# First-parity keys and queries by seven block products ahead of the FFN, values beside FFN chunks 0 and 1

## The chip, the core and the metric

The kernel runs on one core of a Trainium2 chip. The metric is the device time of one execution in microseconds (us); the median of several runs counts. The engines are PE (TensorE: matrix products), DVE (VectorE), ACT (ScalarE), POOL (GpSimd) and SP (SyncE, which only issues transfers). PE reads its operands from on-chip memory (SBUF) and writes sums into eight banks of PSUM of 128 x 512 numbers each; DVE and ACT read and write both.

## What is computed

For 2048 tokens x of 512 channels the kernel mixes an attention with a feed-forward network (FFN). The gate `g` is one number per token.

```python
g = sigmoid((x * gate_w).sum(-1, keepdims=True))
qkv = x @ wqkv                      # 32 heads of 16 channels
idx = pos[:, None] - 2 * arange(8)  # each token looks at 8 tokens, two apart
logits = einsum("bhsd,bhswd->bhsw", q, k[:, :, idx]) * 16 ** -0.5
a = einsum("bhsw,bhswd->bhsd", softmax(logits), v[:, :, idx]) @ wo
b = (gelu(x @ w_gate) * (x @ w_up)) @ w_down      # inner width 1792
out = g * a + (1 - g) * b
```

## The kernel before, in words

Since a token looks only at tokens of its own parity, the 1024 even tokens (parity 0) and the 1024 odd ones (parity 1) are worked through one after the other. Products are made in a 32-bit format of reduced precision, so each operand is split into a high half (a rounded copy, mostly made by ACT) and a low half (what is left, a subtraction, mostly made by DVE); each product of blocks is three matrix products: high by high, low by high, high by low. `split` (L82) does this. PE walks over tiles of 128 tokens (8 in a parity, two blocks of 4) and over the 512 channels in `KC` = 4 chunks.

Opening of parity 0 (L793 to L836). x and the weights of the keys and queries of the first 16 heads (column block 0, "cb 0") are loaded on the queues of SP and ACT and split. PE makes cb 0 with `qkv_mm` (L185): 8 tiles x 4 chunks x 3 = 96 products of 512 columns into eight banks. `take_first` (L196) copies the results from PSUM, half of the copies on ACT and half on DVE, and stores them to DRAM by SP. Then `project(0, 1)` (L223) makes the values (cb 1) for both halves of the heads: 192 products of 256 or 258 columns; ACT copies them and stores them from its own queue, and after the last one L240 to L243 turn the logits z of the gate into g. Beside it run the sums of x that the FFN needs (`sums_x`, L125) and the weights of FFN chunk 0 (`combine`, L420, and `operands`, L429, whose low half is a negated copy on ACT to which a POOL transfer adds the raw weights).

FFN (`ffn`, L623). The inner width is cut into 14 chunks of 128. Gate and up projection of a chunk are a product of 2 x 2 blocks, made with seven block products instead of eight (`gate_up`, L537): sums s1 to s4 of blocks of x, sums t1 to t4 of blocks of the weights; the fourth product of a chunk runs late, in the next chunk (`late`, `fourth`). GELU runs on ACT, the product with the up half on DVE, and the result is split again (`hidden`, L494). The down projection of two chunks is made two chunks later as "pieces" of a chunk (`down`, L510). In chunks 0 and 1, which have no such pieces yet, the pieces are `project_one` (L245): the keys and queries of the other 16 heads (cb 2), 96 products of 512 columns.

Attention (L258 to L386) runs on DVE, for 8 units (4 of each parity): scores, softmax, mix. It is a generator from which the steps of PE's work `pull` a budget (L391), so the order is written by hand. `paced` (L348) ties an instruction's place in the schedule to the last product issued, and the order on each engine is settled when the program is built, by a scheduler with its own estimate of times. Scores of a unit need its keys and queries, softmax needs g, mix needs the values. Loads and stores go through SP's queue, the accumulating ones through POOL's. Parity 1 follows in the same way, then the output projection.

What the prediction's steps touch: the warm-up products (L71), the opening (L793 to L836), `project` and `project_one` (L223, L245), the gates (L240), `gate_up`'s pieces in chunks 0 and 1 (L636), and ACT's work at the passage from chunk 1 to chunk 2 (L442, L447, L471, L474, L570, L586).

## Time and profile before

| | us |
|---|---|
| median of 3 runs | 613.11 (611.63 to 613.8) |
| profiled execution | 612.18 |
| its span, first to last instruction | 610.4 |
| PE busy in the span | 602.1 |
| DVE busy | 515.0 |
| ACT busy | 380.0 |
| POOL busy | 82.8 |

The profile is of one execution. A row of the order of time gives the start (us from the span's first instruction), the duration, the engine, the line of the kernel, the operation, the tile written and the tiles read, the shapes and the number of instructions merged; what stands in brackets is the idle time before it and what ended it. A row of a group has, behind the first bar, the busy time in us and the mean duration of one in ns, behind the second the idle time of the engine just before them. PEld is PE's loading of the fixed operand, which overlaps its products. A busy PE is not a PE at its peak, because products are pipelined and their ends are modelled.

### The profile page before, as it was taken

The page shows a single profiled execution, that of the slowest core. Times are in us where ns is not written, and L with a number is a line of the kernel's source. Part 1 is how long each engine was busy: PE and PEld are TensorE (multiplying, and loading weights), DVE is VectorE, ACT ScalarE, POOL GpSimd, SP SyncE. Part 2 cuts the span into 40 slices and gives each one's busy share as a digit, 9 for nine tenths or more (in the row PEclk, how much of TensorE's full clock was granted, in tenths as well). Part 3 has the DMA queues.
Part 4 walks back from the last instruction along what each step waited for, and adds up shares of the span by engine and source line. Part 5 has one row for each costly group of instructions (what it writes and reads, how often), then busy time and mean ns, then how long its engine had stood idle before and what let it go on. Part 6 is the DMA issues. An engine that isn't in the chain of part 4 may idle for free.

```text
span 610.4 us, 8251 instructions
## 1 busy us (share of the span) xinstructions
PE 602.1 (99%) x2839; PEld 503.6 (83%) x2839; DVE 515.0 (84%) x598; ACT 380.0 (62%) x635; POOL 82.8 (14%) x110
## 2 busy tenths in 40 slices
PE   9999999999999999999999999999999999999996
PEld 7898887888887888888889887888888888888885
DVE  6949686969989788799898898999798979999882
ACT  6654465687677777785375347556865676684722
POOL 0151021121111111101100001111111111101200
PEclk9999999999999999999999999999999999999999
DMA  8398978899979979885579989686877886938615
GB/s 286 116 269 238 308 195 236 250 231 248 263 189 284 238 212 267 222 238 170 188 227 256 315 264 283 159 242 161 246 179 217 204 266 135 274 110 200 88 35 172
DMA packets 85591, 132.48 MB, mean 217 GB/s; under 512 B 8111, under 2 KB 52271, under 8 KB 85550
## 3 DMA queue, kind: packets, MB, share of 16 engines
q1 hardware_dynamic: 63742, 94.27, 47.6%
q0 software_dynamic: 12672, 32.84, 28.7%
q10 hardware_dynamic: 9136, 4.85, 2.7%
q8 instruction: 22, 0.36, 0.3%
q14 instruction: 19, 0.16, 0.1%
HBM read 67.18 MB, written 36.77 MB: 170 GB/s over the span
## 4 chain that ended last, share of the span: by engine, by line
PE 93%; DMA 3%; issue 1%; DVE 1%; ACT 1%; POOL 0%; SPq 0%; POOLq 0%; ACTq 0%
PE p L481 40%; PE acc L191 18%; PE p L521 12%; PE acc L521 12%; PE p L742 5%; PE p L191 4%; PE acc L742 2%; DMA g<-raw 2%; DMA d<-r 1%; DMA raw<-xt 1%; DVE prod L327 0%; ACT g L442 0%; POOL g L443 0%; ACT s L788 0%; ACT lg L307 0%
## 5 line engine op out<-in xcount | busy, mean ns | idle before, releaser
L481 PE MATMUL p<-S,g 128*128 128x512 f32 x672 | 165.7, 389 | 0.0
L481 PEld LDWEIGHTS p<-S,g 128*128 128x128 f32 x672 | 126.1, 188 | 26.2
L481 PE MATMUL p<-A,g 128*128 128x512 f32 x504 | 127.5, 390 | 0.7 <-DMA g<-raw 0.7
L481 PEld LDWEIGHTS p<-A,g 128*128 128x128 f32 x504 | 94.3, 188 | 21.0 <-DMA g<-raw 1.1
L289 DVE TENSOR_TENSOR prod<-kq 128x2048 f32<-128x2048 f32 x32 | 73.2, 2288 | 14.4 <-DMA kq<-kq 5.0
L443 POOL DMA_DIRECT2D g<-raw x42 | 36.3, 864 | 314.8 <-ACT g L442 232.9
L327 DVE TENSOR_TENSOR prod<-v,lg 128x2048 f32<-128x2048 f32 x32 | 73.0, 2281 | 3.9 <-PE p L521 2.1
L292 DVE TENSOR_REDUCE lg<-prod 128x128 f32<-128x2048 f32 x32 | 73.1, 2283 | 0.4
L521 PE MATMUL p<-d,hh 128*128 128x512 f32 x224 | 68.3, 390 | 0.6 <-ACT p L515 0.6
L521 PE MATMUL acc<-d,hh 128*128 128x512 f32 x224 | 59.9, 391 | 0.3 <-DMA d<-r 0.3
L486 ACT ACTIVATE s<-p 128x512 f32<-128x512 f32 x56 | 33.2, 594 | 28.3 <-PE p L481 28.1
L521 PEld LDWEIGHTS acc<-d,hh 128*128 128x128 f32 x224 | 41.9, 188 | 10.1 <-DMA d<-r 1.4
L521 PEld LDWEIGHTS p<-d,hh 128*128 128x128 f32 x224 | 41.9, 188 | 9.7 <-ACT p L515 1.1
L495 DVE TENSOR_TENSOR c<-c 128x512 f32<-128x512 f32 x56 | 38.3, 684 | 11.8 <-ACT c L586 11.2
L442 ACT ACTIVATE g<-raw 128x1024 fp32r<-128x1024 f32 (+1 forms) x42 | 41.3, 982 | 11.2 <-DVE raw L424 9.3
L498 DVE TENSOR_TENSOR hl<-c,hh 128x512 fp32r<-128x512 f32 x56 | 38.4, 685 | 11.1 <-ACT hh L497 10.5
L447 ACT ACTIVATE g<-raw 128x1024 fp32r<-128x1024 f32 (+1 forms) x42 | 41.1, 987 | 9.6 <-PE p L481 9.4
L491 DVE TENSOR_TENSOR c<-p,s 128x512 f32<-128x512 f32 x56 | 38.1, 686 | 10.0 <-PE p L481 10.0
L497 ACT ACTIVATE hh<-c 128x512 fp32r<-128x512 f32 x56 | 35.1, 626 | 16.1 <-DVE c L495 16.0
L521 PE MATMUL p<-d,hl 128*128 128x512 f32 x112 | 42.6, 389 | 0.0
L534 ACT ACTIVATE rt<-p 128x512 f32<-128x512 f32 x48 | 28.2, 594 | 18.8 <-PE p L521 18.2
L331 DVE TENSOR_TENSOR prod<-prod 128x1024 f32<-128x1024 f32 x32 | 39.0, 1220 | 0.4
(147 smaller groups left out, 909.9 us busy)
## 6 DMA issues: line engine op xcount, KB each, us to landing
g<-raw POOLq DMA_DIRECT2D x28, 512.0 KB, 6.0
raw<-wff SPq DMA_DIRECT2D x42, 256.0 KB, 4.1
ws<-g SPq DMA_DIRECT2D x14, 768.0 KB, 5.4
g<-ws SPq DMA_DIRECT2D x14, 768.0 KB, 6.3
r<-wff SPq DMA_DIRECT2D x28, 256.0 KB, 3.9
d<-r POOLq DMA_DIRECT2D x28, 256.0 KB, 6.3
g<-raw POOLq DMA_DIRECT2D x14, 384.0 KB, 4.9
v<-vs SPq DMA_DIRECT2D x8, 512.0 KB, 7.5
```

The source lines that it names most:

```text
L191: LAST[:] = [nc.tensor.matmul(ps[:, :cn], a[:, t], w[:, c0:c0 + cn], start=(kc == 0 and n == 0), stop=(kc == KC - 1 and n == 2))]
L289: paced(nc.vector.tensor_tensor(prod, spans(k, jj), q[:, jj:jj + 2, None, :].to_broadcast([P, 2, W, UC]), op=OP.mult))
L292: nc.vector.tensor_reduce(two_of(lg, jj), prod.rearrange("p j w (h d) -> p (j w) h d", d=DH), axis=AX.X, op=OP.add)
L327: paced(nc.vector.tensor_tensor(prod.rearrange("p j w (h d) -> p (j w) h d", d=DH), spans(v, jj).rearrange("p j w (h d) -> p j w h d", d=D ...
L331: nc.vector.tensor_tensor(prod[:, :, :4], prod[:, :, :4], prod[:, :, 4:], op=OP.add)
L442: nc.scalar.activation(lo, raw, AF.Copy, scale=-1.0)
L447: ins = nc.scalar.activation(hi, raw, AF.Copy)
L481: LAST[:] = [nc.tensor.matmul(ps, w_, a_, start=(start and kc == 0 and n == 0), stop=(kc == 1 and n == 2), skip_group_check=True)]
L495: nc.vector.tensor_tensor(ge, ge, up, op=OP.mult)
L498: nc.vector.tensor_tensor(hl_, ge, hh_.bitcast(F32), op=OP.subtract)
L521: LAST[:] = [nc.tensor.matmul(pp, a[:, ts], w, start=(i == 0 and n == 0 and gr == 0), stop=(i == 1 and n == 2), skip_group_check=True)]
L742: LAST[:] = [nc.tensor.matmul(pa, a, b, start=(first and n == 0), stop=(last and n == 2), skip_group_check=True)]
```

## The change

In the opening of parity 0, keys and queries of all 32 heads are made at once as a product of 2 x 2 blocks (token blocks by channel halves on the x side; channel halves by halves of the heads on the weight side), with seven block products of 24 matrix products each, as in the FFN. `start` holds all of it. The four quarter blocks of the weights are loaded as b11 (two transfers on ACT's queue), b21, b12 and b22 (one of 512 KB each on SP's queue) into tiles that attention uses later. DVE makes t1 to t4 (four subtractions of 128 x 1024) and s1 to s4 (which the FFN uses afterwards), and all of them are split, with the high half on ACT. The partial result U = a11 x b11 is copied by ACT into a second bank, so that a12 x b21 can be added to the copy; results of two further products are kept in SBUF by ACT copies and added by DVE (`join`). The low half of the operands of FFN chunk 0 is now made by DVE.

The order in `start` is: U (first chunk of channels, seven filler products behind its second product, then the rest), a12 x b21, s1 x t1, s2 x t2, s4 x b22, s3 x t3, a22 x t4. The warm-up becomes 16 products of 256 columns. The values of parity 0 take the place of cb 2 as pieces of FFN chunks 0 and 1 (`values`), with the budget for attention that they had before, and the gates follow the last of them. Parity 1 stays as it was.

```diff
-WARM = 31
+WARM = 16
+FILLERS = 7
...
+    def gates(par):
+        nc.scalar.activation(en, z[:, par], AF.Exp, scale=-1.0)
+        nc.vector.tensor_scalar_add(en, en, 1.0)
+        nc.vector.reciprocal(g[:, par], en)
+        nc.vector.tensor_scalar(gc[:, par], g[:, par], -1.0, 1.0, op0=OP.mult, op1=OP.add)
+
+    def values(jj):
+        for hh in range(2):
+            ps = bank(f"acc{(2 * jj + hh) % BT}")
+            qkv_mm(ps, 0, jj, 1, range(KC), (CU, 0)[hh], (WQ, CU)[hh])
+            take(ps, 0, jj, hh, True, tag=None if jj < 5 else "c")
+        pull(2.7)
+        if jj == NP - 1:
+            done.add((0, 1))
+            gates(0)
...
-                pieces = [[lambda jj=jj: project_one(par, jj) for jj in jjs]
+                tile_ = (lambda jj: project_one(1, jj)) if par else values
+                pieces = [[lambda jj=jj: tile_(jj) for jj in jjs]
                           for jjs in (((0, 1), (2, 3), (4, 5), ()), ((6,), (7,), (), ()))[f]]
...
-    project(0, 1, first())
+    def start():
...
+        (xh, xl), (wh, wl) = X[0, 0, 0], KW["b11"][0]
+        mm(U[0], 0, xh, wh, True)
+        mm(U[0], 0, xl, wh)
+        for _ in range(FILLERS):
+            ins = nc.tensor.matmul(U[-1][:, :P], warm[:, :P], warm[:, :P], start=True, stop=True)
...
+        def seed(t):
+            V_.append(bank("p"))
+            nc.scalar.activation(V_[t], U[t], AF.Copy)
+
+        block(U, "a11", "b11", False, seed, (1,))
+        split_x(0, 0, 2)
+        split_x(0, 0, 3)
+        operand("b21", b21, g1b)
...
+        block(V_, "a12", "b21", False, lambda t: put(t, V_[t]))
...
+        for kc in range(2):
+            nc.vector.tensor_tensor(s12[kc], q[kc][2], q[kc][3], op=OP.add)
+            split(nc.vector, *XOP["s1", kc], s12[kc])
+        d = [r for _ in range(4) for r in rooms_of("d", 2)]
+        sub(b11, b12, b11)
+        operand("t1", b11, d[:4])
...
+        block(Z_, "s1", "t1", True, keep_p5)
+        for kc in range(2):
+            sub(s12[kc], s12[kc], q[kc][0])
+            split(nc.vector, *XOP["s2", kc], s12[kc])
+        sub(b11, b22, b11)
+        operand("t2", b11, d[4:])
+        block(U, "s2", "t2", False, keep_u2)
...
+        operand("b22", b22, rooms_of("g0", 3, WA) + rooms_of("c", 1))
...
+        sub(b12, b22, b12)
+        operand("t3", b12, [r for _ in range(3) for r in rooms_of("s", 1)] + rooms_of("c", 1))
+        block(Z_, "s4", "b22", False, lambda t: join(t, Z_[t], u2[t]))
+        sub(b21, b21, b11)
+        operand("t4", b21, g1b)
+        block(U, "s3", "t3", False, lambda t: join(BT + t, U[t], p5[t]))
...
+        block(U, "a22", "t4", False, lambda t: put(BT + t, U[t]))
+        done.update(((0, 0), (0, 2)))
+
+    start()
```

Here `block` runs the 24 matrix products of one block product, tile by tile; `operand` splits 512 columns at a time; `put` is `take_first`; `join` adds the kept partial result and stores keys and queries.

More of the change, by code (lines that the diff above doesn't have):

```diff
@@ L65, in bank @@
         return psum.tile([P, 512], F32, name=tag, bufs=BUFS.get(tag, 1))
[L68 to L80 removed]
+    zero = pool.tile([P, UC], F32, name="zero")
+    nc.vector.memset(zero, 0.0)
+    warm = zero.bitcast(mybir.dt.bfloat16)
+    LAST = []
+    idle = [bank("p") for _ in range(4)]
+    for i in range(WARM):
+        c = i // 4 % 2 * QW
+        LAST[:] = [nc.tensor.matmul(idle[i % 4][:, c:c + QW], warm[:, :P], warm, start=not c, stop=True,
+                                    skip_group_check=True)]
     def split(eng, hi, lo, raw, copy=None):
@@ L790, in finish @@
                 queue.dma_start(out_v[2 * jj + 1, :, c], r[:, c])
-    room = rooms()
-    room_x(0)
-    for kc in range(KC):
-        first = ((0, P), (P, 512 - P)) if not kc else ((0, 512),)
-        sp = load_cb(0, kc, "c", room)
-        if not kc:
-            XR.update((i, tl("raw")) for i in range(2))
-        for blk in range(2):
-            for a, n in first if not blk else ((0, 512),):
-                o = (2 * blk + kc // 2) * 512 + a
-                nc.sync.dma_start(XR[kc % 2][:, o:o + n], xt[blk, :, kc, a:a + n])
-            split_x(0, blk, kc, first if not blk else ((0, 512),), nc.vector.tensor_copy if not (kc or blk) else None)
-            if not blk:
-                sp()
@@ L807, in tile_gated_mix @@
-    ps = [bank(next(names)) for _ in range(NP)]
-    for kc in range(KC):
-        for jj in range(NP):
-            qkv_mm(ps[jj], 0, jj, 0, (kc,))
-    for t in (*KS.values(), *VS.values()):
-        for c in range(2):
-            paced(nc.gpsimd.dma_start(t[c, :W], zero))
-    for jj in range(NP):
-        take_first(ps[jj], jj, nc.vector.tensor_copy if jj % 2 else lambda o, i: nc.scalar.activation(o, i, AF.Copy))
-    done.add((0, 0))
-    for kc in range(KC):
-        load_cb(1, kc, "c", room)()
@@ L829, in first @@
         combine(0)
         for i in range(2):
-            yield
-            for _ in operands(0, 0, i):
-                yield
-        combine(1)
-    project(0, 1, first())
+            n = len(GROUPS[i]) * QW
+            w = tl(f"g{i}", F32R)
+            hi, lo = w[:, :n], w[:, n:2 * n]
+            for k, op in enumerate(GROUPS[i]):
+                WG[0, op] = hi[:, k * QW:(k + 1) * QW], lo[:, k * QW:(k + 1) * QW]
+            split(nc.vector, hi, lo, RAW[0][:, (0, 4)[i] * QW:][:, :n])
```

165 lines of the change are left out of this document (132 added, 33 removed).

## The prediction

> **What bounds the kernel now.** I read the page first: the busy times, then the chain of waits.
>
> ```profile
> span 610.4 us, 8251 instructions
> PE 602.1 (99%) x2839; PEld 503.6 (83%) x2839; DVE 515.0 (84%) x598; ACT 380.0 (62%) x635; POOL 82.8 (14%) x110
> PE 93%; DMA 3%; issue 1%; DVE 1%; ACT 1%; POOL 0%; SPq 0%; POOLq 0%; ACTq 0%
> ```
>
> PE is the bound over the whole span, and 93% of the chain that ended last is PE. So a product less is a gain, and any wait that PE is given is a loss, because nothing later takes it back. Then I cut the first 96 us into the stages that the change touches. The columns are PE, weight loads, DVE, ACT and POOL busy, then clock, DMA share and GB/s.
>
> ```profile
> 4.40:27.50 23.10, 22.59 (x97) 18.18 (x97) 21.20 (x38) 15.23 (x29) 0.00 (x0) 1.00 0.66 221
> 27.50:52.00 24.50, 24.50 (x200) 24.21 (x198) 16.02 (x20) 13.32 (x36) 10.28 (x19) 1.00 0.84 230
> 52.00:84.00 32.00, 32.00 (x143) 26.50 (x142) 25.53 (x24) 13.74 (x21) 2.47 (x3) 1.00 0.93 288
> 84.00:96.00 12.00, 11.67 (x52) 9.30 (x51) 9.64 (x11) 9.16 (x15) 2.60 (x3) 1.00 0.80 184
> ```
>
> The reader should see the first row: while PE makes 96 key and query products, DVE is busy 21.2 of 23.1 us. DVE is nearly full exactly where the change adds DVE work. In the last row ACT is busy 9.2 of 12 us, where before (third row) it had 18 us free.
>
> **The price of a product.** From PE's order of time:
>
> ```profile
> 4.42 0.99 PE L191 MATMUL p<-g,A 128*128 128x512 f32 x2
> 5.91 0.50 PE L191 MATMUL p<-g,A 128*128 128x512 f32 x1 [0.51 <-DVE A L84]
> 16.65 1.52 PE L191 MATMUL p<-S,A 128*128 128x512 f32 x6
> 18.01 1.52 PE L191 MATMUL acc<-S,A 128*128 128x512 f32 x6
> 27.53 1.24 PE L191 MATMUL acc<-g,A 128*128 128x258 f32 x9
> 28.60 0.52 PE L191 MATMUL acc<-c,A 128*128 128x258 f32 x3
> ```
>
> Six 512-column products take 18.01 - 16.65 = 1.36 us, 0.2267 each; nine value products take 1.07, 0.119 each. Keys and queries of the first parity need 192 products before (two heads' halves, 8 token tiles, 4 chunks of channels, 3 for the high and low halves) and 7 x 4 x 2 x 3 = 168 after. **Removed: 24 x 0.2267 = 5.44 us of PE.** The values' 192 products only move. The warm-up (31 of 128 columns, then 16 of 256) is as many columns, and the seven fillers stand in the gap before the row at 5.91, where PE waits for x anyway; I cost both at nothing, -0.2 to +0.3. Without the gap the fillers would cost their own length, under 0.8 us.
>
> **What the opening adds.** The seven products need sums of x and of the weights, and each sum is split in two halves, the high one on ACT and the low one on DVE. The DVE rows that price them:
>
> ```profile
> 6.84 0.69 DVE L87 TENSOR_TENSOR g<-c,g 128x512 fp32r<-128x512 f32 x1
> 13.37 0.68 DVE L87 TENSOR_TENSOR A<-raw,A 128x512 fp32r<-128x512 f32 x1
> 13.97 0.69 DVE L133 TENSOR_TENSOR raw<-raw 128x512 f32<-128x512 f32 x1
> 23.65 0.42 DVE L202 COPY kq<-p 128x256 f32<-128x256 f32 x1
> 23.99 0.41 DVE L203 COPY hl<-p 128x256 f32<-128x256 f32 x1
> L331 DVE TENSOR_TENSOR prod<-prod 128x1024 f32<-128x1024 f32 x32 | 39.0, 1220 | 0.4
> ```
>
> Back to back a 512-wide operation costs 0.60 (13.37 to 13.97), a PSUM copy 0.34, a 1024-wide subtraction 1.22 - 0.08 = 1.14. In the built order of the changed program PE can run 56 products (a11 x b11, a12 x b21, and eight of s1 x t1). The 57th needs the low half of t1 = b12 - b11. On DVE that half stands behind these, counted from the operation that is at 6.84 in both programs: 18 operations of 512 with itself (10.8), the two 1024-wide subtractions t1 and t3 (2.28), and four copies of finished a12 x b21 tiles (1.36). That is 14.4 us if DVE never waits. It waits once for b21, whose arrival I take from these two rows (the second is GB/s in slices of 1.125 us from 0):
>
> ```profile
> 8.27 0.63 ACT L86 ACTIVATE A<-raw 128x512 fp32r<-128x512 f32 x1 [0.99 <-DMA raw<-xt]
> GB/s 0 17 288 249 389 219 339 406 402 380 357 365 316 298 189 0 0 7 0 0 9 232 343 193 154 118 148 276 192 261 259 364 369 371 241 208 204 220 245 259
> ```
>
> The load that ends at 1,280 KB lands at 8.25, and 256 KB more at 400 GB/s are 0.65 us, so b21 lands about 8.9; its high half follows on ACT at 9.5, where DVE would have come at 8.05: 1.5 us, and I add 0.4 for one later wait on ACT. **The half is ready at 6.84 + 14.4 + 1.9 + 0.1 = 23.3 us** (bounds: 21.4 with no wait, 25.0 if DVE waits about as much again). The remaining 112 products take 25.4. PE stands still on the way again: s4 x b22 writes the banks of s1 x t1, and their copies stand on ACT behind a split that waits for DVE (0.6, then 0.3 twice, since a copy is longer than a product), then the high half of t2 (0.5): 1.7, between 0 and 3. Keys and queries end at 23.3 + 25.4 + 1.7 = 50.4.
>
> Both kernels are then compared at the same work. Before, at 52.0, the first half of keys and queries, all values and 6 FFN products are done, and 96 x 0.2267 = 21.8 remain: 73.8. After: 50.4 + 192 x 0.119 (22.9) + 6 x 0.2267 (1.4) = 74.7. **The opening comes out at +0.9**: the 5.44 are spent on waits for DVE. Between the bounds: -2.7 to +3.9. The eight joins (0.60 each), the values' splits and the operands of chunk 0, which change from a POOL DMA to DVE, come after the handover and beside products; they cost nothing as long as DVE is done by about 50, and its queue after 23.3 (some 43 operations, about 27 us) just is. The 18 stores to DRAM on SP and the values' stores on ACT's queue move with their steps; PE waits for neither.
>
> **What the move of the values adds.** The gates need an Exp after the last value. Before, that Exp stood ahead of the FFN; now it stands in chunk 1 between two GELUs, and the softmax's Exp follows. The built order has 21 table loads on ACT instead of 17, three of them at the passage from chunk 1 to 2, where before there was none:
>
> ```profile
> 66.42 1.28 ACT L570 ACT_TABLE_LOAD   x1
> 67.72 0.60 ACT L570 ACTIVATE c<-p 128x512 f32<-128x512 f32 x1
> 50.67 0.21 ACT L240 ACTIVATE en<-z 128x8 f32<-128x8 f32 x1 [0.38 <-ACT z L221]
> 49.84 0.39 ACT L213 ACTIVATE hh<-acc 128x256 f32<-128x256 f32 x1 [1.07 <-PE acc L191]
> 50.12 0.17 ACT L221 ACTIVATE z<-acc 128x1 f32<-128x1 f32 x1
> 63.58 0.62 ACT L307 ACTIVATE lg<-lg 128x512 f32<-128x512 f32 x1
> 83.71 0.60 ACT L586 ACTIVATE c<-p 128x512 f32<-128x512 f32 x1 [0.76 <-PE p L481]
> 88.27 1.79 ACT L447 ACTIVATE g<-raw 128x768 fp32r<-128x768 f32 x2
> L447 ACT ACTIVATE g<-raw 128x768 fp32r<-128x768 f32 x14 | 11.8, 842 | 0.0
> 90.08 1.52 PE L481 MATMUL p<-A,g 128*128 128x512 f32 x6
> 90.28 1.15 ACT L474 ACTIVATE d<-r 128x512 fp32r<-128x512 f32 x2 [0.22 <-PE p L481]
> 91.44 0.39 PE L521 MATMUL acc<-d,hh 128*128 128x512 f32 x1
> 92.16 0.50 PE L521 MATMUL acc<-d,hh 128*128 128x512 f32 x1 [0.33 <-DMA d<-r]
> ```
>
> Before, ACT goes without a break from the GELU at 83.71 to the high halves of chunk 2's operands: the first is ready at 88.27 + 0.84 = 89.1, and PE takes it at 90.08, 1.0 us of room. After, two loads (2.56), the Exp (0.2), a second value copy and z (0.5) stand in between: 3.3 more. PE has 0.6 more work there (24 value products and 19 of 512, 7.2 us, against 29 of 512, 6.6). So PE waits 3.3 - 1.0 - 0.6 = 1.7. Next, PE needs the high half of the down weights. Behind the operands' first half ACT has the third load (1.28), the softmax's Exp (0.53 back to back), the second operand (0.95) and that copy (0.63): 3.4, and PE has six products (1.4) to run: 2.0 more. Less the 0.33 that PE waits at this place already, **the passage costs +3.4**, between 0 and 4.5.
>
> [...]
>
> **The sum.** +0.9 + 3.4 = +4.3 us. The profiled execution took 612.18 (span 610.4 and 1.8 around it), 0.93 under the median of the three runs, 613.11; so 616.5 by that execution and **617.4 us as a median**. 0.3% of it, about what a measurement of this kernel can tell from no change, is 1.84 us.
>
> **The rivals.**
> - *DVE keeps up* (the faster side). If t1's low half were there whenever PE comes, PE would run its third product at about 6.0 (5.91 in the row above, which waits for the same piece of x), ten more by 8.3, the 13th by 8.5, and end keys and queries at 8.5 + 156 x 0.2267 = 43.9, 6.5 earlier: 617.4 - 6.5 = 610.9. For it: DVE only has to hand over one half early, and the order could be other than I count. Against: 18 operations at a measured 0.60. The change gains from the point at which the half is there before 19.0 (23.3 - 4.3). If the passage is hidden as well: 607.5.
> - *The loads fall into ACT's idle time.* ACT was idle 18 us between 52 and 84; if it enters the passage early, only the opening stays: 613.1 + 0.9 = 614.0. Against: at 83.71 ACT waits for PE, so it can't be early.
> - *Attention falls behind.* When PE begins chunk 2, DVE has done 9 of attention's operations of 2.28 us in the built order, and 14 before: a debt of 11 us. DVE is idle 16% of the span, so I expect it repaid beside PE; half of it on the path gives 622.4. The engine orders agree again in the second half, which speaks against it.
> [...]
>
> **How the numbers follow.** Forecast 0.60 (its own range 614.9 to 620, with 0.03 of it below); loads hidden 0.12; DVE keeps up 0.11, both 0.05; attention behind 0.08; double loads 0.04. Faster by over 0.3% (under 611.27): 0.16. Within: 0.12 + 0.03 = 0.15. Slower: 0.69. The range 611.5 to 621.5 leaves out the two faster cases (0.16) and about half of the late attention.
>
> **What would show it.** Right: DVE over 95% busy from 9 to 38 us; PE idle in several pieces of 0.3 to 1.6 us from 12 to 30 us; the 57th product near 23.3, released by DVE; values starting near 50; three table loads within 7 us near 88 to 94, and two PE waits of 1.7 and 2.0 released by ACT there. Wrong: values starting before 46 (then the DVE count fails); no wait for ACT before chunk 2; PE waits after 100 us that before doesn't have.

## The result, and the profile after

The changed kernel takes **623.0 us** in the median of six runs (619.14 to 625.28), the kernel before 612.66 in six runs: ratio 1.0173, 95% interval 1.0152 to 1.0195. It is slower, as forecast, but by 10.3 us in place of 4.3, and outside the range. The six go with the granted clock: 0.997 at 619.14, 0.996 at 621.23, 0.991 at 622.88 and 623.13, 0.986 to 0.989 at 625. The profiled execution, 625.28, is the slowest of the six. From its page:

```profile
span 623.5 us, 8204 instructions
PE 605.4 (97%) x2807; PEld 502.3 (81%) x2807; DVE 527.6 (85%) x617; ACT 387.4 (62%) x647; POOL 81.1 (13%) x108
PE 88%; issue 6%; DMA 3%; DVE 1%; ACT 1%; POOL 0%; SPq 0%; POOLq 0%
```

PE has 32 instructions fewer (2807 for 2839: 24 products and 15 of the warm-up less, seven fillers more), and yet is busy 3.3 us longer (605.4 for 602.1): its products have become slower. Where, the stages show (columns as in the prediction: PE, weight loads, DVE, ACT, POOL, clock, DMA share, GB/s):

```profile
4.40:51.10 46.70, 43.26 (x177) 32.85 (x176) 41.37 (x69) 28.36 (x55) 9.30 (x17) 0.96 0.61 198
51.10:88.00 36.90, 36.90 (x255) 34.30 (x254) 22.87 (x18) 17.25 (x40) 2.58 (x3) 1.00 0.73 206
88.00:103.00 15.00, 9.83 (x37) 7.04 (x36) 9.93 (x15) 9.90 (x15) 1.74 (x2) 0.94 1.00 279
130.00:140.00 10.00, 6.43 (x22) 4.86 (x21) 5.53 (x9) 4.09 (x6) 0.86 (x1) 0.77 1.03 257
```

The last two stretches in the kernel before:

```profile
88.00:103.00 15.00, 14.67 (x65) 11.76 (x65) 9.68 (x11) 9.34 (x15) 3.13 (x4) 1.00 0.91 237
130.00:140.00 10.00, 10.00 (x46) 8.29 (x45) 7.57 (x11) 8.00 (x14) 2.59 (x3) 1.00 1.01 237
```

PE stands still 3.4 us in the opening (4.40 to 51.10), 5.2 at the passage into chunk 2 (88 to 103) and 3.6 at 130 to 140, and in these three stages the granted clock is below 1. The DMA share of the last two is 1.00 and 1.03; before it was 0.91 and 1.01, at full clock. PE's own rows:

```profile
18.69 1.66 PE L886 MATMUL p<-d,S 128*128 128x512 f32 x6 [1.02 <-ACT d L86]
21.31 0.70 PE L886 MATMUL p<-d,S 128*128 128x512 f32 x2 [0.95 <-DVE hl L201]
23.02 5.37 PE L886 MATMUL p<-d,S 128*128 128x512 f32 x16 [1.01 <-DVE d L87]
...
93.61 1.66 PE L490 MATMUL p<-A,g 128*128 128x512 f32 x6 [1.61 <-ACT g L456]
97.02 1.20 PE L530 MATMUL acc<-d,hh 128*128 128x512 f32 x4 [1.75 <-ACT d L483]
100.04 0.50 PE L530 MATMUL acc<-d,hh 128*128 128x512 f32 x1 [1.81 <-DMA d<-r]
...
136.36 2.08 PE L490 MATMUL p<-A,g 128*128 128x512 f32 x4 [3.57 <-DMA g<-raw]
```

The first five waits are of the kinds forecast; the third, fourth and fifth are the very ones (the low half of t1, and the two at the passage). The last two are not: they end with an accumulating transfer of POOL. The one before 136.36, issued at 126.30, took 10.0 us to land; the same one of the kernel before took 3.8 (KB each, median us from issue to landing; after, then before):

```profile
g<-raw POOLq DMA_DIRECT2D x1, 384.0 KB, 10.0
```

```profile
g<-raw POOLq DMA_DIRECT2D x1, 384.0 KB, 3.8
```

Just ahead of it stand attention's loads of keys and queries for the third unit, 1.47 MB, on SP at 123.67 to 124.51; before, the same loads went out at 104.15 to 107.94. Half the clock was granted in three places (the last is two stretches of 3.41 us long):

```profile
22.76:26.17 3.41, 3.15 (x7) 2.48 (x8) 3.41 (x7) 1.06 (x3) 3.41 (x8) 0.50 0.38 91
101.27:104.68 3.41, 3.41 (x9) 2.64 (x8) 3.41 (x5) 0.00 (x0) 0.00 (x0) 0.50 1.03 367
135.40:142.23 6.83, 5.87 (x14) 4.62 (x15) 1.32 (x4) 3.67 (x6) 0.00 (x0) 0.50 0.93 276
```

**An account of PE's time.** For each profiled execution: the time from the start of the first real product to a point, less the price of the products issued between (0.2267 per 512 columns and 0.119 per value product, from the prediction's rows; 0.107 per filler of 256 columns, as 24 of them took 2.55 us in e1_fill). What is left is lost, to waits or to half clock, up to 50 us, from 50 to 105, from 105 to 150, and later. In the row of e1_fill the fillers count as products, so the 8.1 us that they fill are not in its losses. Each row of losses is one execution, which can lie up to 2.3 us from its median (the changed kernel's 625.28, e2_gates' 619.17). The kernel before was run again beside each group of experiments, and took 611.94 to 613.04.

| kernel | median (95% interval of the ratio to before) | lost to 50 | 50-105 | 105-150 | later |
|---|---|---|---|---|---|
| before | 612.66 | 1.6 | 0.7 | 0.4 | 2.7 |
| changed | 623.0 (1.0152-1.0195) | 8.3 | 7.9 | 6.6 | 1.3 |
| e1_fill | 618.57 (1.0083-1.0127) | 5.5 | 2.0 | 1.0 | 0.9 |
| e2_gates | 621.33 (1.0117-1.0181) | 7.5 | 5.4 | 3.3 | 1.8 |
| e3_low | 621.74 (1.0124-1.0168) | 7.2 | 1.9 | 5.0 | 3.8 |
| e4_order | 618.25 (1.0077-1.0117) | 6.2 | 5.1 | 5.3 | 0.5 |
| e5_hold | 618.41 (1.0079-1.0117) | 7.2 | 5.6 | 0.2 | 4.0 |
| e6_all | 618.01 (1.0066-1.0127) | 6.5 | 5.7 | 0.0 | 2.7 |
| e7_ahead | 612.75 (0.9999-1.0020) | 7.2 | 3.1 | 1.6 | 0.3 |
| e8_plain | 617.51 (1.0046-1.0098) | 1.8 | 9.2 | 0.1 | 0.7 |
| e9_both | 614.97 (1.0032-1.0061) | 1.7 | 3.1 | 0.5 | 2.7 |
| e10_between | 621.25 (1.0121-1.0155) | 2.4 | 6.4 | 3.6 | 7.3 |
| e11_pull8 | 616.59 (1.0054-1.0088) | 1.9 | 4.9 | 6.1 | 4.5 |
| e12_trans | 618.93 (1.0073-1.0130) | 7.7 | 2.5 | 2.3 | 5.1 |
| e13_noload | 616.56 (1.0040-1.0082) | 7.5 | 2.3 | 2.9 | 2.2 |
| e14_bnoload | 614.61 (1.0021-1.0059) | 1.4 | 5.0 | 5.0 | 1.0 |
| e15_spread | 622.06 (1.0126-1.0175) | 2.2 | 6.5 | 3.0 | 9.8 |
| e16_spread4 | 618.37 (1.0050-1.0100) | 1.9 | 5.0 | 5.0 | 5.4 |
| e17_four | 613.31 (0.9994-1.0025) | 1.9 | 2.2 | 2.5 | 4.0 |
| e18_four54 | 616.21 (1.0032-1.0081) | 1.7 | 5.4 | 1.3 | 6.5 |

The products after cost 5.1 less (24 x 0.2267, less seven fillers of about 0.05, half of 0.107); the losses add up to 24.1 against 5.4. The difference, 13.6, is close to that of the two spans, 13.1. It is more than the 10.3 us between the medians, because the profiled execution is the slowest of its six.

### The profile page after: what moved, and what is told of

It reads as the page before. It is cut to its first block, busy times and chain, and to the rows that moved or that the text cites. A ratio compares the mean times of both kernels' runs of the same rounds, so it can differ in the third digit from the quotient of the medians.

```text
span 623.5 us, 8204 instructions
## 1 busy us (share of the span) xinstructions
PE 605.4 (97%) x2807; PEld 502.3 (81%) x2807; DVE 527.6 (85%) x617; ACT 387.4 (62%) x647; POOL 81.1 (13%) x108
## 4 chain that ended last, share of the span: by engine, by line
PE 88%; issue 6%; DMA 3%; DVE 1%; ACT 1%; POOL 0%; SPq 0%; POOLq 0%
PE p L490 40%; PE acc L189 13%; PE p L530 11%; PE acc L530 11%; PE p L752 5%; PE acc L886 3%; PE p L886 2%; PE p L189 2%; PE acc L752 2%; DMA g<-raw 2%; DMA prod<-wqkv 1%; ACT p L899 0%; ACT A L86 0%; POOL d L481 0%; POOL g L452 0%
## 5 line engine op out<-in xcount | busy, mean ns | idle before, releaser
L490 PE MATMUL p<-S,g 128*128 128x512 f32 x672 | 169.4, 394 | 0.0
L490 PEld LDWEIGHTS p<-S,g 128*128 128x128 f32 x672 | 128.2, 191 | 27.3 <-ACT s L495 0.2
L452 POOL DMA_DIRECT2D g<-raw x40 | 34.7, 868 | 335.7 <-ACT g L451 196.3
L507 DVE TENSOR_TENSOR hl<-c,hh 128x512 fp32r<-128x512 f32 x56 | 38.3, 683 | 10.6 <-ACT hh L506 10.2
L456 ACT ACTIVATE g<-raw 128x1024 fp32r<-128x1024 f32 (+1 forms) x40 | 39.5, 989 | 11.8 <-PE p L490 11.5
L451 ACT ACTIVATE g<-raw 128x1024 fp32r<-128x1024 f32 (+1 forms) x40 | 39.4, 984 | 3.5 <-DVE raw L433 2.2
```

Of the source, the lines that this page charges most:

```text
L451: nc.scalar.activation(lo, raw, AF.Copy, scale=-1.0)
L456: ins = nc.scalar.activation(hi, raw, AF.Copy)
L490: LAST[:] = [nc.tensor.matmul(ps, w_, a_, start=(start and kc == 0 and n == 0), stop=(kc == 1 and n == 2), skip_group_check=True)]
L507: nc.vector.tensor_tensor(hl_, ge, hh_.bitcast(F32), op=OP.subtract)
```

## The experiments

The theory after the result: the opening's and the passage's waits are the forecast ones; beyond them, transfers land late because attention's loads, 20 us later than before, meet them, and every longer wait is followed by a stretch of half clock. The rivals: the clock falls for another reason; the transfers are late for one of their own. All runs are variants of the changed kernel unless said otherwise. The diffs are excerpts; `...` stands for lines left out.

**e1_fill: hold the clock, take no wait away.**

```diff
+    def fillers(ps, n, start):
+        for _ in range(n):
+            ins = nc.tensor.matmul(ps[:, :QW], warm[:, :P], warm, start=start, stop=True, skip_group_check=True)
+            paced(ins)
...
+        if not par and f == 2:
+            fillers(X_, 12, True)
```

> The changed kernel (623.0 us in the median) with 76 products of zeros added on TensorE in five places where it waited: 8 + 8 around the second product of the opening, 12 ahead of chunk 2, 12 + 12 around the first 'down' products, 24 ahead of the product of chunk 4 that waited for its accumulating transfer until 136.36. No wait is taken away; the zeros are added to banks and change no sum. Theory A (the records show TensorE at half clock at 22.76-26.17, 101.27-104.68 and 135.40-142.23 because it had stood idle just before; this costs 1.75 + 1.7 + 2.9 = 6.4 us beside the waits themselves): the three stretches are at full clock, the granted clock rises from 0.989 to about 0.999, and the time is 616.6 to 618.5 us, ratio to the kernel before 1.007 to 1.010. Rival B (the clock falls there for another reason, such as the transfers beside it, or the slow products only take time out of waits that would follow anyway): the time stays at 621 to 624, ratio 1.014 to 1.019. Rival C (fillers delay the products behind them): above 624.

618.57: just above theory A's range (616.6 to 618.5). At the very times of the half clock above, 15, 17 and 32 products are started in place of 7, 9 and 14, all of them real ones:

```profile
22.76:26.17 3.41, 3.38 (x15) 2.80 (x16) 3.41 (x6) 1.06 (x3) 3.41 (x7) 1.00 0.33 86
101.27:104.68 3.41, 3.41 (x17) 2.83 (x16) 3.41 (x5) 2.26 (x4) 0.51 (x1) 1.00 0.99 364
135.40:142.23 6.83, 6.83 (x32) 5.64 (x31) 6.19 (x12) 6.20 (x9) 1.79 (x3) 1.00 1.03 318
```

So about 4.4 of the 10.3 us (623.0 - 618.57) is the clock behind the waits. The transfers beside it did not make it fall here: at shares of 0.99 and 1.03 it stayed at 1.00.

**e2_gates: two table loads fewer at the passage.**

```diff
-            gates(0)
...
-        nc.scalar.activation(lg, lg, AF.Exp, scale=DH ** -0.5)
+        ins = nc.scalar.activation(lg, lg, AF.Exp, scale=DH ** -0.5)
+        if not (par or u):
+            gates(0, ins)
```

> The changed kernel with one thing moved: the Exp of the gates stands directly behind the Exp of the first softmax on ScalarE, no longer between two Gelus, so two of the 21 table loads fall away and the passage from chunk 1 to chunk 2 holds two loads in place of three pairs. Theory A (three loads at 87.57, 90.94 and 93.58 made the two waits of 1.61 and 1.75 us, as predicted): the wait at 93.61 goes, the one at 97.02 shrinks to 1.5 or less, the one of 1.81 at 100 for the transfer stays or grows to 2.5; 1.3 to 2.5 us less, and 1.7 more where the stretch at half clock at 101 goes with them: 619 to 621.7 us, ratio 1.011 to 1.015. Rival B (the transfer d<-r that landed at 100 sets the end of this passage whatever ScalarE does): the time that is saved ahead of it is waited again at it, 622.3 to 623.5, ratio 1.016 to 1.018.

621.33, the number of A, but not clear of the changed kernel: the intervals of the two overlap, and the six runs fall into two groups, 619.17 to 619.65 and 623.01 to 624.55. The profile is of the fastest. In it the wait for the operand is gone, and so is the one for the transfer at 100, which A had left; the one for the down weights is still 1.84, and a new one stands behind it:

```profile
94.49 1.19 PE L534 MATMUL acc<-d,hh 128*128 128x512 f32 x4 [1.84 <-ACT d L487]
96.77 2.93 PE L494 MATMUL p<-S,g 128*128 128x512 f32 x6 [1.09 <-DVE c L504]
```

The passage loses 5.4 in place of 7.9, with one stretch of half clock in both (in e2_gates six products took 2.93 us at 96.77, and 1.52 at 101.65): in these two executions the edit takes a third of it away.

**e3_low: no POOL transfer for the late operands.**

```diff
+        if f == 4 and not (par or i):
+            KEEP[f] = w[:, :2 * n]
+            paced(nc.scalar.activation(hi, raw, AF.Copy))
+            nc.vector.tensor_tensor(lo, raw, hi.bitcast(F32), op=OP.subtract)
...
+        if f in LOWS:
+            LOWS.remove(f)
+            paced(nc.scalar.activation(d[:, :512], rd, AF.Copy))
+            nc.vector.tensor_tensor(d[:, 512:1024], rd, d[:, :512].bitcast(F32), op=OP.subtract)
+            yield
+            return
```

> The changed kernel with three accumulating transfers of GpSimd taken out: the low halves of the weights d of chunks 0 and 1 and of the first operand group of chunk 4 are subtracted by VectorE (2 x 0.69 and about 1.0 us of it). Theory A (these transfers landed 9 to 10 us after their issue in place of 4.5 to 5.3 because attention's loads of keys and queries now go out just ahead of them; TensorE waited 1.81 us at 100.04 and 3.57 at 136.36, and lost 1.7 + 2.9 more at half clock behind them): both waits and both stretches of half clock go, 7 to 10 us less: 613 to 616 us, ratio 1.001 to 1.006. Rival B (the next transfers in the queue, those of the second group, are as late and wait in their place): 2 to 4 us of it come back, 616.5 to 620. Rival C (VectorE has no room, and the subtractions come as late as the transfers): 621 to 624.

621.74: A is wrong about the time and right about the passage (1.9 lost in place of 7.9; a negated copy on ACT goes as well, which may be part of it). As rival B said, the second group was late in place of the first, and as C said, DVE had to be waited for:

```profile
96.71 3.06 PE L503 MATMUL p<-S,g 128*128 128x512 f32 x12 [1.35 <-DVE c L513]
133.22 3.77 PE L503 MATMUL p<-A,g 128*128 128x512 f32 x10 [1.80 <-DMA g<-raw]
```

**e4_order: DVE's order in the opening.** The subtractions for s4, s3 and t3 and the split of b22 wait for tiles 2 and 3 of s1 x t1.

```diff
-            sub(q[kc][1], q[kc][1], s12[kc])
+            sub(q[kc][1], q[kc][1], s12[kc], mark[3])
...
-        operand("b22", b22, rooms_of("g0", 3, WA) + rooms_of("c", 1))
+        operand("b22", b22, rooms_of("g0", 3, WA) + rooms_of("c", 1), mark[2])
```

> The changed kernel with VectorE's work in the opening put into another order: the subtractions for s4, s3 and t3 and the split of b22 are held until tiles 2 and 3 of the product s1 x t1, so that the low half of t1 comes as soon as its high half is there. Theory A (the queue of VectorE, which did 6 other groups ahead of it, made the product wait until 23.02): the three waits of 1.02, 0.95 and 1.01 us fall to 1.0 or less in sum, the half clock at 22.76 goes (1.75 us), and some 1 to 1.5 us come back later in the opening, where VectorE has the rest still to do: 2 to 3.5 us less, 619.5 to 621 us, ratio 1.011 to 1.014. Rival B (VectorE's total work sets the end of the opening, in any order): the values begin at 51.1 as now, 622.3 to 624.

618.25, better than A said. The opening did what A said:

```profile
19.55 4.42 PE L897 MATMUL p<-d,S 128*128 128x512 f32 x18 [0.21 <-DVE hl L201]
43.42 5.74 PE L897 MATMUL acc<-g,A 128*128 128x512 f32 x24 [0.73 <-DVE hh L949]
48.99 1.24 PE L189 MATMUL acc<-d,A 128*128 128x258 f32 x9
```

The three waits are one of 0.21, the half clock at 22.76 is gone (clock 1.00 from 20 to 51 us), and 1.4 us come back later (0.17, 0.51 and 0.73) where DVE's work comes due. The values begin at 48.99 in place of 51.12, so B falls. At full clock the order alone is worth 1.0 us (7.2 lost in e5_hold, 6.2 here). The rest of the 4.75 us is mostly half clock that did not come, in the opening and at the passage (clock 1.00 from 88 to 103 us). There PE still waited 2.55 and 1.75 us, so not every longer wait was followed by half clock.

**e5_hold: attention's loads out of the way of one transfer.**

```diff
+            if to and jj == HOLD:
+                load_kq(*to, held=True)
...
-            if ahead:
+            late_ = to if un == (0, 0) else None
+            if ahead and not late_:
                 load_kq(*to)
```

> The changed kernel with one thing moved: attention's three loads of keys and queries for its third unit (1.47 MB), issued at 123.67 to 124.51 us ahead of GpSimd's accumulating transfer of 126.30, are held until the middle of the first unit's mix, some 15 us later. Nothing else is touched. Theory A (these loads made that transfer land after 10 us in place of 5, so that TensorE waited 3.57 us until 136.36 and then ran 6.8 us at half clock): the wait falls to 0.5 us or less and the half clock behind it goes: 4 to 6.4 us less, 616.6 to 619 us, ratio 1.007 to 1.011; the passage at 93 to 104 us is as before. Rival B (the transfer is late for a reason of its own, such as the stores of the values or the queue of GpSimd): the wait at 136 stays over 2.5 us and the time is 621.5 to 624. Rival C (the loads meet the next transfers where they now stand): a wait of 2 us or more near 150, 619 to 622.

618.41, as A said: nothing but the loads was moved, the transfer for chunk 4 landed in 5.2 us in place of 10.0, and PE lost 0.2 us from 105 to 150 in place of 6.6. Part of it came back 24 us later (rival C, at another place). And part of the gain is not the moved loads': in this execution no half clock followed the waits of the opening and of the passage either (clock 1.00 from 20 to 51 and from 88 to 103 us; A had the passage as before), and PE lost 1.1 and 2.3 us less there. The transfer, and the wait 24 us later:

```profile
g<-raw POOLq DMA_DIRECT2D x1, 384.0 KB, 5.2
```

```profile
162.15 1.19 PE L500 MATMUL p<-A,g 128*128 128x512 f32 x4 [2.33 <-DMA g<-raw]
```

**e6_all: the edits together** (e2, e4, e5 and the first half of e3).

> The changed kernel with four of the edits at once: VectorE's order in the opening (617.8 to 619.7 us by itself), the gates' Exp behind the first softmax's, the low halves of d of chunks 0 and 1 by VectorE, and the loads of keys and queries of unit 2 held as in the run beside it. Theory A (the 24 products fewer are worth 5.4 us once the waits that the change brought and the half clock behind them are gone): no wait over 1 us between 45 and 200 us, granted clock 0.998 or more, 606 to 611 us, ratio 0.990 to 0.998, faster than both kernels. Rival B (new waits of the same size come up elsewhere, with attention 20 us behind where it was): 611.5 to 617, ratio 0.999 to 1.008.

618.01, outside A and B. The gains do not add up. The passage still lost 5.7, now mostly at one wait of 2.83 for an addition on DVE (97.81) and the half clock behind it (0.89 on average from 88 to 103 us).

**e7_ahead, e8_plain, e9_both: each part undone, and both.**

```diff
-                tile_ = (lambda jj: project_one(1, jj)) if par else values
+                tile_ = (lambda jj: project_one(1, jj)) if par else lambda jj: None
...
+    for jj in range(NP):
+        values(jj)
     ffn(0)
```

```diff
-        block(Z_, "s1", "t1", True, keep_p5)
...
+        block(U, "a11", "b12", True, None)
+        block(U, "a12", "b22", False, lambda t: other(t, U[t]))
+        block(Z_, "a21", "b11", True, None)
+        block(Z_, "a22", "b21", False, lambda t: put(BT + t, Z_[t]))
...
+        block(U, "a21", "b12", True, None)
+        block(U, "a22", "b22", False, lambda t: other(BT + t, U[t]))
```

> The changed kernel with the values' move undone: the eight tiles of values are computed between the seven products and the FFN, and the first two chunks of the FFN have nothing between their products. Theory A (values beside chunk 1 put the gates' pair of table loads and the values' copies on ScalarE right at the passage into chunk 2): the waits of 1.61, 1.75 and 1.81 us there and the half clock go, a wait or two of up to 1.5 us come at the short chunks 0 to 2, whose operands have 9.5 us for their transfers; 2 to 5 us less, 618 to 621 us, ratio 1.009 to 1.014; the wait at 136 and its half clock may stay. Rival B (the products of the values beside the chunks were cover for the operands' transfers, and without them each of chunks 1 and 2 waits for its own): 623 to 628.

> The changed kernel with the seven products undone: the first parity's keys and queries are made by eight block products (192 in place of 168 products of TensorE, 5.44 us more), at the same place, with the values beside chunks 0 and 1 as in the change. Theory A (the seven products gave their 5.44 us back in the opening: three waits on ScalarE and VectorE of 3.0 us, a half clock of 1.75, and some smaller ones, so the opening netted +0.7): the values begin at 50 to 52 us in place of 51.1, no wait of TensorE over 0.6 us between 7 and 50 us, and the time is 620 to 623.5 us, ratio 1.012 to 1.018, though TensorE has 24 products more. Rival B (the seven products do gain, and all the loss lies in the values' move): 625.5 to 628, ratio 1.021 to 1.025.

> The changed kernel with both parts undone: eight block products (24 products of TensorE more, 5.44 us) and the values ahead of the FFN, with nothing between the products of chunks 0 and 1. It completes the square of the two parts: both 623.0 us, values undone 612.75, seven products undone 617.5. Theory A (the seven products earn nothing, since VectorE's handover in the opening takes 5.4 us back): beside the kernel with the values undone it is the same within 1 us: 611.8 to 613.8, ratio 0.9995 to 1.003. Rival B (the seven products earn their 5.4 us once the values stand ahead of the FFN): 616.5 to 619, ratio 1.007 to 1.011. Rival C (the seven products lose 5 us in themselves, as the comparison with the values beside the chunks says): 606.5 to 609.

612.75, 617.51 and 614.97. The opening with seven products, then with eight (e7_ahead, e8_plain):

```profile
20.00:51.00 31.00, 28.41 (x124) 22.32 (x124) 28.86 (x49) 16.53 (x31) 7.12 (x14) 1.00 0.60 172
```

```profile
20.00:51.00 31.00, 31.00 (x139) 25.66 (x138) 19.10 (x33) 11.52 (x21) 7.16 (x14) 1.00 0.57 158
```

With eight, PE never stops and DVE is busy 19.1 of 31 us; with seven, DVE is busy 28.9 and PE loses 7.2 - 1.8 = 5.4 us more, which is all that 24 products are worth. So the seven products earn nothing in the opening, as Theory A of e8_plain had it. Where the rest differs it is the values: ahead of the FFN, the kernel with seven products is 10.2 us faster than with the values beside the chunks. That is far more than A of e7_ahead said. And e8_plain is faster than either theory: the late transfer at 136 is not there (0.1 us lost from 105 to 150), and why not was not tested. e9_both is 2.2 slower than e7_ahead, between A and B. The two openings balance (5.4 + 1.7 against 7.2), so that lies later, where each version has waits of its own; the largest of the square stand at the passage of e8_plain, 9.2 us:

```profile
91.90 1.65 PE L490 MATMUL p<-S,g 128*128 128x512 f32 x6 [2.41 <-ACT s L495]
98.22 2.07 PE L490 MATMUL p<-A,g 128*128 128x512 f32 x4 [4.67 <-ACT g L456]
```

So the two parts hurt each other: with the values ahead of the FFN seven products are 2.2 us faster than eight, with the values beside the chunks 5.5 us slower.

**e12_trans: late transfers dealt with, values beside the chunks** (first half of e3 and e5).

> The changed kernel as it is, values beside chunks 0 and 1 and seven products, with only the late transfers dealt with: the low halves of d of chunks 0 and 1 by VectorE, and the loads of keys and queries of unit 2 held as before; GpSimd's transfers for chunk 4 are left. Theory A (what the values' move lost beyond the opening is the late transfers, the wait for ScalarE that belongs to d's low half, and the half clock behind them): the passage loses about 2 us in place of 8, the wait at 136 is gone, and 612.5 to 616 us are left, ratio 1.001 to 1.006. Rival B (the transfers are only the last of several queues that are late together at the passage, and another comes in their place): 616.5 to 620.

618.93, as rival B said. The passage lost 2.5, near the 2 that A expected, and other waits took over: 2.04 for DVE at 97.53 and 2.33 for a transfer at 160.03.

**e10_between, e11_pull8: cover for DVE's handover.**

```diff
-        pull(2.7)
+        pull(0.0 if jj < BT else 5.4)
...
+        for jj in range(4):
+            values(jj)
...
         sub(b11, b12, b11)
-        operand("t1", b11, d[:4])
+        operand("t1", b11, rooms_of("g1", 4))
```

The other four tiles of values stand between the opening and the FFN, and attention's share beside the values goes to them.

> The seven products kept, the values ahead of the FFN, and the values of the first four tiles moved between the second and the third of the seven products, where VectorE is behind: 10.9 us of TensorE's work that need only what is split already, and their weights loaded ahead of the second token block. Theory A (in the opening TensorE waits only for VectorE's handover of the low halves, 5.4 us in all, because the third product comes before VectorE has done its part; cover at that place gives them back): no wait over 0.5 us between 18 and 50 us, and the 24 products fewer count in full: 5 us less than the kernel with the values undone, 606 to 609 us, ratio 0.990 to 0.995, faster than both kernels. Rival B (VectorE's total work sets the end of the opening, whatever stands between): the waits come back at the later products, 610.5 to 613, ratio 0.998 to 1.002. Rival C (attention, pushed back by another 5 us, ends last): a wait of several us in the last 30 us, over 613.

> The run with the values of four tiles between the second and third product, with attention's share beside the last four tiles of values raised from 5.4 to 8.0 us each, so that attention stands where it stood before the move. Theory A (attention is not on the path): within 1.5 us of that run. Rival B (attention's place decides at the end of the kernel): 1.5 us or more faster than it.

In e10_between the opening did what A said; the time, 621.25, did not. The opening's row, and what came after it:

```profile
20.00:51.00 31.00, 31.00 (x177) 27.26 (x176) 25.23 (x39) 15.61 (x37) 8.38 (x16) 1.00 0.46 136
```

```profile
79.46 3.06 PE L490 MATMUL p<-S,g 128*128 128x512 f32 x12 [1.36 <-DVE c L500]
90.81 1.20 PE L490 MATMUL p<-A,g 128*128 128x512 f32 x4 [2.40 <-DMA g<-raw]
...
143.63 2.58 PE L490 MATMUL p<-A,g 128*128 128x512 f32 x10 [1.94 <-DMA g<-raw]
```

PE loses 2.4 us in the opening, with all 24 products saved, and 17 later. With more of attention early (e11_pull8) it is 616.59, 4.7 us faster, the number of rival B: attention's place matters, though not as B had it, since PE has no wait for it at the kernel's end.

**e13_noload, e14_bnoload: without attention's loads.** Units 1 to 3 of parity 0 work on unit 0's tiles.

```diff
+        if not par and u:
+            LG[0, u] = OLD["kq"]
+            return
```

> The changed kernel without attention's loads for units 1 to 3 of the first parity (keys, queries and values, 2.4 MB a unit): they work on unit 0's tiles, so their attention is not the reference's; every other instruction is there. Theory A (these loads make GpSimd's accumulating transfers late): no wait of TensorE for an accumulating transfer over 0.5 us, the waits of 1.81 and 3.57 and the half clock behind them gone: 612.5 to 617 us, ratio 1.000 to 1.007. Rival B (attention's work on VectorE, which now runs without a pause, delays the FFN's additions): waits for VectorE come in their place, 618 to 622.

> The kernel with four tiles of values between the second and the third product (621.25 us), without attention's loads for units 1 to 3 of the first parity, as in the run beside it. Theory A (loads against transfers): the waits for transfers at 90.8, 143.6, 189.9 and 206.9 (2.40, 1.94, 0.91 and 1.77 us) and the half clock behind two of them go, 9 to 11 us less: 609.5 to 613 us. Rival B (VectorE's queue): the waits for it at 79.5 and 110.6 stay and grow, 615 to 621.

616.56 and 614.61: 6.4 us under the changed kernel and 6.6 under e10_between. The loads are a large part of the loss, but not all of it. The first time is inside A, and the waits of 1.81 and 3.57 are gone; but one of 1.55 for a transfer stands at 128.56, where A had none over 0.5. The second lies just under rival B's range and above A's. What stayed in e14_bnoload:

```profile
90.55 1.21 PE L495 MATMUL p<-A,g 128*128 128x512 f32 x4 [2.45 <-DMA g<-raw]
128.00 2.56 PE L495 MATMUL p<-A,g 128*128 128x512 f32 x10 [2.65 <-DMA g<-raw]
```

**e15_spread, e16_spread4: attention thinner at first** (2.7 or 4.0 us beside each of four tiles, 0.97 or 0.93 beside the FFN, for 5.4 and 0.90).

> The kernel with four tiles of values between the second and the third product, all loads there, with attention's share beside the other four tiles of values halved to 2.7 us each and its share beside the FFN's first pass raised from 0.90 to 0.97 of TensorE's time. Theory A (loads against transfers): the waits for transfers stay, in other places, at 4 us or more in sum: 615 to 620 us. Rival B (attention too thick on VectorE at 57 to 110 us): the waits there fall under 1 us and the opening's gain comes through: 608 to 613 us, faster than or equal to the kernel before. Rival C (attention ends last): over 620, with a wait in the last 30 us.

> As the run beside it, with 4.0 us beside each of the four tiles and 0.93 beside the FFN, between that run and the one with 5.4 and 0.90 (621.25). Theory A: 615 to 621, by where the loads fall. Rival B: between the two runs, 611 to 618.

622.06 and 618.37: B falls, and the first is above A too. The waits near 79 (1.36 to 1.63) and near 91 (2.40 to 2.45) are much the same for any share of attention and without its loads (e10, e11, e14, e15, e16), so neither causes them. e15_spread adds a wait of 4.31 for ACT at 266.50. What these five kernels have in common is chunks 0 and 1 with nothing between their products. That alone does not make the waits as long: e7_ahead has the same empty chunks, and waits 0.73 and 0.81 us at 85 and 93.

**e17_four, e18_four54: clean opening, last four tiles of values beside chunks 0 and 1.** The diff is that of e17_four against e10_between; the gates' Exp moves as in e2_gates, and attention's share beside the FFN is 0.93.

```diff
-            pull(0.0 if jj < BT else 5.4)
+            pull(0.0 if jj < BT else 4.0)
...
-                tile_ = (lambda jj: project_one(1, jj)) if par else lambda jj: None
+                tile_ = (lambda jj: project_one(1, jj)) if par else values
...
-                          for jjs in (((0, 1), (2, 3), (4, 5), ()), ((6,), (7,), (), ()))[f]]
+                          for jjs in ((((0, 1), (2, 3), (4, 5), ()), ((6,), (7,), (), ())) if par else (((4,), (5,), (), ()), ((6,), (7,), (), ())))[f]]
```

> Seven products, four tiles of values between the second and the third of them, the other four beside chunks 0 and 1 (two each), the gates' Exp directly behind the first softmax's, attention's share 4.0 us beside each of the four tiles and 0.93 beside the FFN. Theory A (values beside the chunks cover the operands' transfers, and what the change lost at the passage was the table loads): the waits at 79 and 90 go, 3.9 us and a half clock of 1.7: beside the run with the same shares and empty chunks (618.4) 4 to 6 us less, 611 to 615 us, ratio 0.997 to 1.004. Rival B (the passage costs the same wherever the values stand): 616 to 620. If the waits for late transfers near 110 to 210 stay away too, 606 to 610.

> As the run beside it, with attention's share 5.4 us beside each of the four tiles and 0.90 beside the FFN. Theory A: the waits at 79 and 90 go here too, 612 to 617 us (the run with these shares and empty chunks took 621.25). Rival B: 618 to 622.

613.31 and 616.21, both as A said. The wait at 79 is gone in both; e18_four54 has 2.17 at 90.21 for another transfer, e17_four these:

```profile
86.40 1.66 PE L494 MATMUL p<-A,g 128*128 128x512 f32 x6 [0.76 <-ACT g L460]
88.94 0.50 PE L534 MATMUL acc<-d,hh 128*128 128x512 f32 x1 [0.58 <-DMA d<-r]
109.19 1.19 PE L534 MATMUL acc<-d,hh 128*128 128x512 f32 x4 [1.52 <-DMA d<-r]
212.49 1.65 PE L494 MATMUL p<-A,g 128*128 128x512 f32 x6 [1.26 <-ACT rt L547]
```

Beside the runs with the same shares and empty chunks both are 5 us faster (e16_spread4 618.37, e10_between 621.25). So values beside the chunks are not bad in themselves: they serve as cover, as far as two runs that also move the gates' Exp can show it. e17_four is 9.7 us faster than the changed kernel and can't be told from the kernel before (ratio 1.0009, 0.9994 to 1.0025). No version here beats the kernel before.

## Why the prediction was wrong

- **Products: right.** 24 fewer (2807 PE instructions, 2831 in e8_plain), 5.44 us by their price.
- **Opening, +0.9: right in its mechanism, and near in size where the clock was full.** The 57th product came at 23.02 (forecast 23.3), released by DVE. The 1.7 us of smaller waits behind it came too: in e2_gates, at full clock there, the last 112 products take 50.27 - 23.01 = 27.26 us, 1.9 over their price of 25.4. The brackets show only 0.24 and 0.37 of it; the rest lies in products that start 0.49 us after the one before them in place of 0.2267. In the changed kernel the half clock of 22.76, which the step did not count, came on top: the first 16 of the products took 5.37 us, 3.93 in e1_fill. The values began at 51.12 (forecast 50.4; 49.9 to 50.4 in e1_fill, e2_gates, e3_low and e5_hold, where the first 16 took 3.92 to 3.94 us). By the account the opening came out at 8.3 - 1.6 - 5.1 = +1.6, and with e5_hold's 7.2 at +0.5.
- **Passage, +3.4: the two waits right, the step short.** 1.61 and 1.75 came where 1.7 and 2.0 were forecast, behind three table loads. The step counted neither the transfer for d (1.81) nor the half clock of 101.27. The loss there is 7.9 - 0.7 = 7.2 us.
- **The sum, +4.3: the step that failed.** It added waits at their own length and took the rest of the kernel as it was. Between 105 and 150 PE lost 6.6 - 0.4 = 6.2 us more than before, for which the sum had nothing. "PE waits after 100 us that before doesn't have" was the mark of a wrong forecast, and it came. Two things were left out: behind waits that left PE idle for 50, 53 and 76% of a stretch of 3.41 us the granted clock fell to 0.50 (4.4 us in all; in e1_fill, with products of zeros at the waits, it was 1.00 at those times), and attention's loads move with attention and meet transfers that PE waits for (without the loads the changed kernel is 6.4 us faster, e13_noload; that is the price of the loads in it and not of their move alone, since the kernel before has them too). The two overlap, as the late transfers made some of the long waits, so they are not to be added. By stages, the profiled execution lost 1.6 us in the opening, 7.2 at the passage and 6.2 from 105 to 150, and 1.4 less than before later.
- **Rivals.** "Attention falls behind" had the nearest time, 622.4 (half of its 11 us on 617.4 would be 622.9), by luck, for a wrong reason: its debt was priced as work on DVE that PE might wait for at the end. PE paid for it at 100 and 136 us through transfers. "DVE keeps up" and "loads in idle time" did not happen. The 0.04 for double loads rests on a price that no run shows: a table load cost its row once (1.28 us at 93.58, the Exp at 94.87).

What stays open: with a clean opening (e10_between, e17_four) 5 us should be left over, and they were lost again, mostly between 50 and 300 us, in every arrangement. The runs name the waits; they show that attention's loads cause part of them, and that values beside chunks 0 and 1 take part of them away. That the rest comes from DVE and the transfers having little slack beside the FFN (DVE is busy 85% of the span) is argued, not shown.

## What to carry to other kernels

Price a saving on the bounding engine together with what the earlier or later work does to shared queues: here 5.4 us of products were handed back by DVE within the opening, and a 20 us shift of attention moved its loads onto transfers that another part needs on time. Gains of single edits did not add up here; and a sum of waits alone came out too low, since half clock followed some of them (4.4 us here). A square of the parts (each undone, both undone) told in three runs what the edits of single waits had not.

## What the runs showed of the hardware

In the trace of the changed kernel the three places at half clock begin at 22.76, 101.27 and 135.40 us, 23 and 10 times 3.413 us apart, and last 3.41, 3.41 and 6.83 us. From the changed kernel, four stretches of 3.41 us with the clock still at 1, three of them just ahead of those places, and one of e4_order:

```profile
19.35:22.76 3.41, 1.71 (x7) 0.78 (x5) 3.41 (x7) 1.50 (x3) 3.41 (x7) 1.00 0.51 143
94.43:97.85 3.42, 1.67 (x8) 1.04 (x6) 1.23 (x1) 3.41 (x6) 0.00 (x0) 1.00 1.10 239
97.85:101.27 3.42, 1.60 (x7) 1.05 (x6) 3.42 (x6) 0.12 (x1) 0.00 (x0) 1.00 1.05 332
131.98:135.40 3.42, 0.82 (x4) 0.35 (x2) 3.42 (x6) 0.66 (x2) 0.00 (x0) 1.00 1.09 243
```

```profile
88.29:91.70 3.41, 1.59 (x8) 0.97 (x6) 2.27 (x7) 3.38 (x6) 1.73 (x2) 1.00 1.04 269
```

PE was busy 1.71, 1.60 and 0.82 us ahead of the three places at half clock; 1.67 and, in e4_order, 1.59 were followed by full clock. So of these five stretches those 50, 53 and 76% idle came before half clock, those 51 and 53% idle before full clock. In e1_fill, with 76 products of zeros added (8.1 us of PE at 0.107), the clock was 1.00 at those times and the median 4.4 us lower. The accumulating transfer of 384 KB for chunk 4 landed in 3.8 us in the kernel before, 5.2 with the loads held (e5_hold), and 10.0 behind 1.47 MB of loads.
